# Batch 1 of a retention-and-mixer kernel: all token blocks mixed by token and turned by DMA, its last chunk closer, and one chunk's loads later in SyncE's queue

## The chip, the cores and the metric

The kernel runs on one core of a Trainium2 chip. The metric is the device time of one execution in microseconds. Every time below is of one core; the TensorE clock granted in the profiled execution was 1.000 of full speed.

## What is computed

Two stages in a row. The first is a recurrent attention over 4 batches, 8 heads, 768 tokens and 64 channels a head: a state of 64 x 64 per head decays by gamma at each token. The second mixes the tokens through a rank of 32 and then applies a two-layer MLP (512 to 2048 to 512) to every token.

```python
def _attn_ref(q, k, v):
    gamma = 1.0 - 2.0 ** (-5.0 - np.arange(H))
    for t in range(S):
        state = gamma[None, :, None, None] * state + np.einsum('bhd,bhe->bhde', k[:, :, t], v[:, :, t])
        y[:, :, t] = scale * np.einsum('bhd,bhde->bhe', q[:, :, t], state)

def _moe_ref(x, U, V, w_ch1, w_ch2):
    xt = x.transpose(0, 2, 1)
    h = xt @ U @ V
    u = x + h.transpose(0, 2, 1)
    ch = np.maximum(u @ w_ch1, 0.0) @ w_ch2
    return u + ch
```

x is the attention's output with the heads side by side (768 tokens x 512), the inputs q, k, v are float32, and so is the output.

## The kernel before

**Tiles and stages.** The 768 tokens of a batch are six chunks (or token blocks) of 128. The attention of a chunk takes the decay into q and k (GpSimd: kd at L250, qd at L255), turns both (qkT, channels on partitions), forms the scores of the chunk (ret_S: 8 matmuls, then two masks a on VectorE, L440), adds the product with the state of the chunks before (ret_O, with x cast on ScalarE, L459), and carries the state on (L478, VectorE). Batches 0 and 1 turn q and k on TensorE (ret_T, L418), batches 2 and 3 by DMA transposes (ret_T_dma, L281, two to a chunk, on SyncE's queue).

**The mixer.** mix_P forms P = U^T x (six matmuls). u = x + V^T P exists in two forms. By token (mix_n): one matmul of 512 columns on TensorE, an add of x on VectorE into the float32 tile res (L530), a cast to bf16 on ScalarE (L532), and one DMA transpose of 128 x 512 into the tile uT on SyncE's queue (L534). By channel (mix_u): three turns of x and one matmul of P and V (384 columns) accumulate one channel block of uT for three token blocks in PSUM, and one eviction writes it; then the residual u is formed again at the end of MLP2 (in mlp2 one more matmul of Vb and P_sb of 512 columns, and x added). by_token(b, j) says which form token block j of batch b takes: in the kernel before, batch 0 none, batch 1 blocks 3 to 5, batches 2 and 3 all.

**The MLP.** MLP1 makes 32 pieces of gT (16 row blocks m times 2 halves of 384 tokens, four matmuls of 384 columns each, 0.65 us). For b > 0 the list of slots starts with eight pieces of the first half of tokens and then eight of the second. mlp1_two runs two pieces together, channel blocks 0 and 1 of both first, then 2 and 3. MLP2 makes, for each of six token blocks j, 16 matmuls of 512 columns in eight slots of two; the last adds the residual on VectorE (L575) and stores 128 x 512 from SyncE (L578).

**What sets the order.** Every engine runs its own instructions strictly in the order of the program. The loop over b at the end of the program builds the main list: MLP1(b), 32 slots, then MLP2(b), 48 slots; n1 is the first slot of MLP2. Into it go, at slots given by hand, the attention of batch b + 1 (at: the turns, S_at: the scores, O_at: the outputs) and its mixer (mix_at: mix_P two slots later, then mix_n and mix_u). For batch 1 these slots lie in MLP2 of batch 0, for batches 2 and 3 in MLP1 and the first part of MLP2 of the batch before. Which of ScalarE and VectorE evicts a piece is chosen while the program is built, by an estimate of their loads (Balance.pick).

**SyncE's queue** holds, in program order, the loads of k, q and v (load_one, L135, 256 KB each), the stores and all DMA transposes; an instruction that waits holds up all behind it. Loads of batch b + 1 are issued at the places of ret_in (batch 1's chunks named in EARLY load one chunk of batch 2 each) and at slots 0, 7 and 15 of MLP1.

Of the kernel before, what the change touches and what calls it, by code (L numbers as in the profile page):

```python
# [47 lines left out]
def kernel(  # L48
# [14 lines left out]
    NCK = S // P  # L63
# [4 lines left out]
    NCB = DM // P  # L68
# [37 lines left out]
    def mm_bank(who="main"):  # L106
        if use[who] is None:
            who = "main"
        b = use[who][n_use[who] % len(use[who])]
        n_use[who] += 1  # L110
        taken[b] = n_bank[0]
        return bank(b)

    def matmul(o, l, r, cols, **kw):
        nc.tensor.matmul(o, l, r, **kw)  # L115
        bal.mm(cols)

    def evict(o, i, cols, relu=False, dve_rate=1.0):
        if bal.pick(cols, dve_rate) == "A":
            nc.scalar.activation(o, i, AF.Relu if relu else AF.Copy)  # L120
        elif relu:
            nc.vector.tensor_relu(o, i)
        else:
            nc.vector.tensor_copy(out=o, in_=i)  # L124
# [13 lines left out]
    def load_chunk(b, c, kinds="kqv"):  # L138
        t = staged.setdefault((b, c), {})
        for nm in kinds:  # L140
            load_one(t, b, c, {"k": k, "q": q, "v": v}[nm], nm + "_n")
# [26 lines left out]
    for what in ("q0", "kA", "q1", "k2", "k3", "vA", "q2", "k4", "v2", "k5", "v3", "v4", "v5"):  # L168
        src, i = {"q": q, "k": k, "v": v}[what[0]], what[1]
# [83 lines left out]
    def ret_q(b, c, eng):  # L253
        qd = rmid.tile([P, H, D], bf16, tag="qd", name=f"qd_{b}_{c}", bufs=4)
        eng.tensor_tensor(qd, rc[b, c]["q_n"], Gq[:, c].unsqueeze(2).to_broadcast([P, H, D]),  # L255
                          op=ALU.mult)
        rc[b, c]["qd"] = qd
# [5 lines left out]
        rc[b, c]["vb"] = vb  # L263


    EARLY = (2, 3, 4)

    def ret_in(b, c):
        ret_k(b, c, nc.gpsimd)
        ret_q(b, c, nc.gpsimd)  # L270
        if b == 1 and c in EARLY:
            load_chunk(b + 1, c - EARLY[0])

# [223 lines left out]
    def mix_x(b, hf, c, bk=None):  # L497
        pieces[b, hf, c] = piece = (mm_bank("mix") if bk is None else bank(bk))[:, :HS]
        for jj in range(HS // P):
            j = hf * (HS // P) + jj  # L500
            matmul(piece[:, ts(jj, P)], xs[b][:, j, ts(c, P)], ident, P, start=(jj == 0),
                   stop=False, skip_group_check=True)

    def mix_h(b, hf, c):
        piece = pieces.pop((b, hf, c))
        matmul(piece, Ps[b][:, ts(c, P)], Vb[:, ts(hf, HS)], HS, start=False, stop=True,
               skip_group_check=True)
        evict(uTs[b][:, c, ts(hf, HS)], piece, HS)

    def mix_u(b, hf, c):  # L510
        mix_x(b, hf, c)
        mix_h(b, hf, c)
# [3 lines left out]
    res = {}  # L516

    def by_token(b, j):
        return b >= 2 or (b == 1 and j >= NCK // 2)

    def res_of(b):
        if b not in res:
            res[b] = resp.tile([P, NCK, DM], fp32, tag="res", name=f"res_{b}")
        return res[b]

    def mix_n(b, j):
        h = mm_bank("mix")
        matmul(h, Vb[:, ts(j, P)], Ps[b], DM, start=True, stop=True)
        u = res_of(b)[:, j]
        nc.vector.tensor_tensor(u, h, xs[b][:, j], op=ALU.add)  # L530
        bal.book("V", 0.69)
        nc.scalar.activation(xs[b][:, j], u, AF.Copy)  # L532
        bal.book("A", 0.63)
        nc.sync.dma_start_transpose(out=uTs[b][:, :, ts(j, P)], in_=xs[b][:, j])  # L534
# [11 lines left out]
    def mlp1_two(b, ms, hf):  # L546
        if b not in gTs:
            gTs[b] = gtp.tile([P, NM, S], bf16, tag="gT", name=f"gT_{b}")
        g = [mm_bank()[:, :HS] for _ in ms]
        for cs in ((0, 1), (2, 3)):  # L550
            for m, o in zip(ms, g):
                for c in cs:
                    matmul(o, w1b[:, c, ts(m, P)], uTs[b][:, c, ts(hf, HS)], HS, start=(c == 0),
                           stop=(c == NCB - 1))
        for m, o in zip(ms, g):
            evict(gTs[b][:, m, ts(hf, HS)], o, HS, relu=True)
# [43 lines left out]
    def put(side, i, f):  # L600
        side.setdefault(int(i), []).append(f)
# [17 lines left out]
    def mix_side(b, i, side):  # L619
        put(side, i + 2, lambda: mix_P(b))  # L620
        js = [j for j in range(NCK) if by_token(b, j)]
        for n, j in enumerate(js):
            put(side, i + 5 + n, lambda j=j: mix_n(b, j))
        if b == 1:
            for c in range(NCB):
                put(side, i + 5 + len(js) + c, lambda c=c: mix_u(b, 0, c))
        return side


# [55 lines left out]
    for b in range(B):  # L685
        nxt = b + 1 < B
        slots = mlp1_slots(b)
        n1 = len(slots)
        side = {}
        set_banks([0, 1, 2, SA, SB, OB])  # L690
        if b == 0:
            taken.update({i: n for n, i in enumerate((1, 2, 0, OB, SA, SB, TP))})
            set_banks([1, 2, 0, OB, SA, SB, TP])
            slots[:4] = [lambda: mlp1_two(0, (0, 1), 0), lambda: None,
                         lambda: mlp1_two(0, (0, 1), 1), lambda: None]
            for i, s in ((1, 2), (2, 3)):
                put(side, i, lambda s=s: load_w1(512 * s, 512))
            for s in range(4):
                put(side, 4 + s, lambda s=s: load_w2(s))
            for c, nm in ((0, "kq"), (1, "kq"), (2, "kq"), (0, "v"), (3, "kq"), (1, "v"), (4, "kq"),  # L700
                          (2, "v"), (3, "v"), (5, "kq"), (4, "v"), (5, "v")):
                put(side, 14, lambda c=c, nm=nm: load_chunk(1, c, nm))
            at, lead, mix_at = [n1 + 7 + 5 * c for c in range(NCK)], 4, n1 + 38
            S_at = {(0, 1): n1 + 14, (2, 3): n1 + 24, (4,): n1 + 30, (5,): n1 + 35}
            O_at = [n1 + i for i in (19, 22, 29, 32, 35, 38)]
        if b:

            slots = slots[:16:2] + slots[1:16:2] + slots[16:]
        if b == 1:
            slots[:2] = [lambda: mlp1_two(1, (0, 1), 0), lambda: None]  # L710
        if b and nxt:
            set_banks([0, 1, 2])
            at, lead, mix_at = [10 + 4 * c for c in range(NCK)], 5, n1 + 25
            S_at = {(0, 1): 27, (2, 3): 37, (4, 5): 47}
            O_at = [32, 35, 43, 46, 53, 56]
        if nxt:
            ret_side(b + 1, at, lead, S_at, O_at, side)
            put(side, n1, lambda: set_banks([0, 1], [2]))
            put(side, mix_at, lambda: use.update(mix=[2, SA, SB, OB]))
            mix_side(b + 1, mix_at, side)  # L720
        if b in (1, 2):
            for c, i in ((3, 0), (4, 7), (5, 15)):
                put(side, i, lambda c=c: load_chunk(b + 1, c))
        weave(slots + mlp2_slots(b), side)

# [29 lines left out]
```

## Time and profile before

| | |
|---|---|
| median of 3 runs | 226.94 us (226.93 to 226.95) |
| the profiled execution's own time | 226.93 us |
| its span, first to last instruction | 225.2 us |
| VectorE, ScalarE, GpSimd busy | 38%, 50%, 26% of the span |
| DMA moved | 34.85 MB, 155 GB/s over the span |
| DMA transposes | 15 into uT, 24 into qkT |

How to read the rows that follow: a row of the timeline gives the start in us from the span's first instruction, how long it lasts, the engine (PE is TensorE, PEld its weight load, DVE VectorE, ACT ScalarE, POOL GpSimd, SPq the issue of a DMA by SyncE), the source line, the operation, what is written and read, how many were merged (x), and in brackets the idle time before with what ended it. A matmul's time runs from its issue to its modelled end, and the next one starts before that end, so the distance of starts is what a matmul costs. An SPq row is the time that SyncE is held by the issue, not the transfer; the transfer's end is given by the time "to landing". DMA share is the mean busy share of the core's 16 DMA engines, where overlapping packets can make more than 1.

### The profile page before, as it was taken

What the parts mean: (1) busy time and instruction counts of PE and PEld (TensorE: products, weight loads), DVE (VectorE), ACT (ScalarE), POOL (GpSimd) and SP (SyncE); (2) the same over time, 40 slices, a digit from 0 to 9 for tenths busy, and PEclk for the clock granted to TensorE, in tenths of its full rate; (3) what the DMA queues carried; (4) which work ended last, traced back from release to release, by engine and by line L of the source; (5) the groups of instructions that cost most, each with busy time, mean ns of one, the idle gap of its engine ahead of it and who ended that gap; (6) DMA issues with size and microseconds to landing.
All of it is one profiled execution on the core that took longest, in us unless ns stands there. A gap on an engine that the chain in (4) does not pass through costs nothing.

```text
span 225.2 us, 4288 instructions
## 1 busy us (share of the span) xinstructions
PE 219.7 (98%) x1735; PEld 124.7 (55%) x1735; DVE 85.4 (38%) x163; ACT 112.0 (50%) x220; POOL 58.9 (26%) x66
## 2 busy tenths in 40 slices
PE   7998999999999999999999999999999999999994
PEld 2466655655656466556554456565554455654454
DVE  8597630003777450034673610045674410001221
ACT  3377657751355277767133547776323467760000
POOL 6756920046643431431035103330000000000000
PEclk9999999999999999999999999999999999999999
DMA  6998999999899999989499669995311580001212
GB/s 172 243 265 181 162 189 199 198 223 226 186 232 219 234 232 206 201 168 127 101 210 243 196 134 231 174 187 97 93 49 57 131 143 0 0 3 47 88 52 95
DMA packets 100772, 34.85 MB, mean 155 GB/s; under 512 B 87152, under 2 KB 97808, under 8 KB 100752
## 3 DMA queue, kind: packets, MB, share of 16 engines
q1 hardware_dynamic: 94640, 30.29, 66.0%
q0 software_dynamic: 6112, 4.29, 13.0%
q8 instruction: 13, 0.21, 0.4%
q14 instruction: 7, 0.06, 0.1%
HBM read 27.46 MB, written 6.29 MB: 150 GB/s over the span
## 4 chain that ended last, share of the span: by engine, by line
PE 90%; DMA 3%; POOL 2%; DVE 1%; ACT 1%; SPq 0%; issue 0%; ACTq 0%
PE bk L115 88%; DMA in<-in_q_dram 3%; POOL qd L304 1%; PE bk L418 1%; ACT st L292 1%; PE bk L311 1%; DVE a L345 1%; SPq L165 0%; POOL kd L299 0%; DVE kT L294 0%; PE bk L323 0%; DVE vb L294 0%; DVE res L575 0%; ACTq L292 0%
## 5 line engine op out<-in xcount | busy, mean ns | idle before, releaser
L115 PE MATMUL bk<-w2b,gT 128*128 128x512 bf16 (+2 forms) x416 | 92.0, 363 | 0.0
L115 PE MATMUL bk<-uT,w1b 128*128 128x384 bf16 x512 | 84.3, 326 | 0.0
L120 ACT ACTIVATE gT<-bk 128x384 bf16<-128x384 f32 x123 | 60.4, 491 | 31.8 <-PE bk L115 31.8
L115 PEld LDWEIGHTS <-w1b 128*128 128x128 bf16 x512 | 49.9, 98 | 33.3 <-issue 0.2
L115 PEld LDWEIGHTS <-gT 128*128 128x128 bf16 x416 | 37.9, 98 | 37.8 <-issue 0.8
L250 POOL TENSOR_TENSOR kd<-k_n,Gk 128x512 bf16<-128x512 f32 x18 | 18.8, 1042 | 77.8 <-DMA k_n<-in_k_dram 58.7
L440 DVE TENSOR_TENSOR a<-bk,mask 128x512 bf16<-128x512 f32 x36 | 22.4, 683 | 36.0 <-PE bk L115 35.8
L575 DVE TENSOR_TENSOR res<-bk,res 128x512 f32<-128x512 f32 (+2 forms) x17 | 10.6, 626 | 44.6 <-PE bk L115 44.6
L459 ACT ACTIVATE x<-bk 128x512 bf16<-128x512 f32 x18 | 10.7, 595 | 23.3 <-PE bk L115 23.3
L255 POOL TENSOR_TENSOR qd<-q_n,Gq 128x512 bf16<-128x512 f32 x18 | 18.8, 1042 | 6.8 <-DMA qkT<-qd 3.4
L478 DVE TENSOR_TENSOR state<-bk,bmask 128x512 bf16<-128x512 f32 x15 | 10.4, 691 | 10.7 <-PE bk L115 10.7
L261 ACT ACTIVATE vb<-v_n 128x512 bf16<-128x512 f32 x18 | 10.8, 622 | 5.8 <-DMA v_n<-in_v_dram 5.8
L530 DVE TENSOR_TENSOR res<-bk,x 128x512 f32<-128x512 f32 x15 | 9.7, 685 | 8.4 <-PE bk L115 8.4
L532 ACT ACTIVATE x<-res 128x512 bf16<-128x512 f32 x15 | 9.3, 630 | 7.1 <-DVE res L530 6.9
L115 PEld LDWEIGHTS <-qkT 64*128 64x128 bf16 (+1 forms) x204 | 8.4, 95 | 7.1 <-issue 3.2
L115 PE MATMUL bk<-idle 128*128 128x512 bf16 x29 | 10.3, 499 | 1.2 <-DVE idle L179 1.2
L124 DVE COPY qkT<-bk 128x1024 bf16<-128x1024 bf16 x3 | 2.1, 691 | 23.9 <-PE bk L418 23.9
L115 PE MATMUL bk<-vb,a 128*128 128x64 bf16 (+1 forms) x208 | 10.1, 193 | 0.0
L115 PE MATMUL bk<-P_sb,Vb 128*128 128x512 bf16 x24 | 9.1, 380 | 0.0
L115 PEld LDWEIGHTS <-a 128*128 128x128 bf16 (+1 forms) x208 | 8.5, 97 | 0.7
L115 PE MATMUL bk<-vb,kd 128*128 128x128 bf16 (+1 forms) x88 | 8.2, 219 | 0.2 <-DVE vb L294 0.2
L345 DVE TENSOR_TENSOR a<-bk,mask 128x512 bf16<-128x512 f32 x12 | 7.7, 684 | 1.4 <-PE bk L115 1.4
(85 smaller groups left out, 132.0 us busy)
## 6 DMA issues: line engine op xcount, KB each, us to landing
out_dram<-res SPq DMA_DIRECT2D x23, 256.0 KB, 2.4
k_n<-in_k_dram SPq DMA_DIRECT2D x22, 256.0 KB, 5.0
v_n<-in_v_dram SPq DMA_DIRECT2D x22, 256.0 KB, 5.0
q_n<-in_q_dram SPq DMA_DIRECT2D x18, 256.0 KB, 5.1
w2b<-in_moe_w_ch_dram POOLq DMA_DIRECT2D x4, 512.0 KB, 15.0
in<-in_q_dram SPq DMA_DIRECT2D x3, 512.0 KB, 6.3
w1b<-in_moe_w_ch_dram POOLq DMA_DIRECT2D x4, 256.0 KB, 6.0
w1b<-in_moe_w_ch_dram POOLq DMA_DIRECT2D x2, 512.0 KB, 9.2
```

The lines of the kernel that those rows point to most:

```text
L115: nc.tensor.matmul(o, l, r, **kw)
L120: nc.scalar.activation(o, i, AF.Relu if relu else AF.Copy)
L250: eng.tensor_tensor(kd, k_n, Gk[:, c].unsqueeze(2).to_broadcast([P, H, D]), op=ALU.mult)
L255: eng.tensor_tensor(qd, rc[b, c]["q_n"], Gq[:, c].unsqueeze(2).to_broadcast([P, H, D]), op=ALU.mult)
L261: nc.scalar.activation(vb, rc[b, c]["v_n"], AF.Copy)
L345: nc.vector.tensor_tensor(r0["a", c][:, e], r0["s", c][e].rearrange("p (n t) -> p n t", n=NP), mask0[:, c].unsqueeze(1).to_broadcast([P, N ...
L440: nc.vector.tensor_tensor(r["a"][:, e], r["s"][e].rearrange("p (n t) -> p n t", n=NP), mask4, op=ALU.mult)
L459: nc.scalar.activation(xs[b][:, c], o, AF.Copy)
L478: nc.vector.tensor_tensor(sb, ps.rearrange("p (n t) -> p n t", n=NP), bmask4, op=ALU.mult)
L530: nc.vector.tensor_tensor(u, h, xs[b][:, j], op=ALU.add)
L532: nc.scalar.activation(xs[b][:, j], u, AF.Copy)
L575: nc.vector.tensor_tensor(o, chp.pop((b, j)), o if by_token(b, j) else xs[b][:, j, ds(lo, w)], op=ALU.add)
```

## The change

Four things change. (1) by_token takes all six blocks of batch 1: blocks 0 to 2 go through mix_n as 3 to 5 did, the four mix_u of batch 1 are gone, and MLP2 of batch 1 adds the finished u instead of forming it again with a matmul for blocks 0 to 2. The two paired MLP1 pieces at the start of MLP1 of batch 1 are single ones again. (2) The last chunk of batch 1 comes earlier: turn at slot n1 + 31 (32 before), scores and the output of chunk 4 at n1 + 34 (35), the output of chunk 5 at n1 + 36 (38). (3) mix_at goes from n1 + 38 to n1 + 36 and the first mix_n follows four slots behind instead of five. (4) The loads of chunk 2 of batch 2 leave the place of batch 1's chunk 4 and go to slot 0 of MLP1 of batch 1, chunk 3's from slot 0 to slot 2.

```diff
-    EARLY = (2, 3, 4)
+    EARLY = (2, 3)
...
     def by_token(b, j):
-        return b >= 2 or (b == 1 and j >= NCK // 2)
+        return b >= 1
...
         for n, j in enumerate(js):
-            put(side, i + 5 + n, lambda j=j: mix_n(b, j))
-        if b == 1:
-            for c in range(NCB):
-                put(side, i + 5 + len(js) + c, lambda c=c: mix_u(b, 0, c))
+            put(side, i + (4 if b == 1 else 5) + n, lambda j=j: mix_n(b, j))
...
-            at, lead, mix_at = [n1 + 7 + 5 * c for c in range(NCK)], 4, n1 + 38
-            S_at = {(0, 1): n1 + 14, (2, 3): n1 + 24, (4,): n1 + 30, (5,): n1 + 35}
-            O_at = [n1 + i for i in (19, 22, 29, 32, 35, 38)]
+            at, lead, mix_at = [n1 + i for i in (7, 12, 17, 22, 27, 31)], 4, n1 + 36
+            S_at = {(0, 1): n1 + 14, (2, 3): n1 + 24, (4,): n1 + 30, (5,): n1 + 34}
+            O_at = [n1 + i for i in (19, 22, 29, 32, 34, 36)]
...
-        if b == 1:
-            slots[:2] = [lambda: mlp1_two(1, (0, 1), 0), lambda: None]
...
-            for c, i in ((3, 0), (4, 7), (5, 15)):
+            for c, i in ((2, 0), (3, 2), (4, 7), (5, 15)) if b == 1 else ((3, 0), (4, 7), (5, 15)):
                 put(side, i, lambda c=c: load_chunk(b + 1, c))
```

SyncE's queue at the end of MLP2 of batch 0, before. res_901 is batch 0's output, x_1008 and uT_1288 are batch 1's, k_n_2 to v_n_4 are chunks 2 to 4 of batch 2:

```order
L135 DMA k_n_2_1069<-in_k_dram 128x8x64
L135 DMA q_n_2_1071<-in_q_dram 128x8x64
L135 DMA v_n_2_1073<-in_v_dram 128x8x64
L578 DMA out_dram<-res_901 128x512 x3
L534 DMA_TRANSPOSE uT_1288<-x_1008 128x4x128 x3
L578 DMA out_dram<-res_901 128x512
L135 DMA k_n_3_1349<-in_k_dram 128x8x64
L135 DMA q_n_3_1351<-in_q_dram 128x8x64
L135 DMA v_n_3_1353<-in_v_dram 128x8x64
L135 DMA k_n_4_1402<-in_k_dram 128x8x64
L135 DMA q_n_4_1404<-in_q_dram 128x8x64
L135 DMA v_n_4_1406<-in_v_dram 128x8x64
```

The same place in the changed kernel (res_901 is still batch 0's output, uT_1276 batch 1's):

```order
L578 DMA out_dram<-res_901 128x512 x3
L534 DMA_TRANSPOSE uT_1276<-x_1008 128x4x128 x6
L578 DMA out_dram<-res_901 128x512
L135 DMA k_n_2_1334<-in_k_dram 128x8x64
L135 DMA q_n_2_1336<-in_q_dram 128x8x64
L135 DMA v_n_2_1338<-in_v_dram 128x8x64
L135 DMA k_n_3_1353<-in_k_dram 128x8x64
L135 DMA q_n_3_1355<-in_q_dram 128x8x64
L135 DMA v_n_3_1357<-in_v_dram 128x8x64
L135 DMA k_n_4_1393<-in_k_dram 128x8x64
L135 DMA q_n_4_1395<-in_q_dram 128x8x64
L135 DMA v_n_4_1397<-in_v_dram 128x8x64
```

Three transposes more stand between the stores, and the three loads of chunk 2 moved from ahead of the stores to behind the transposes; in both kernels the four transposes of q and k of batch 2's chunks 0 and 1 follow, then chunk 5's loads and the transposes of chunks 2 to 5.

VectorE at the same place, before (state_4 is the last state of batch 1, res_1299 its u by token):

```order
L478 TENSOR_TENSOR state_4_1251<-bk_95_1018,bmask 128x512
L575 TENSOR_TENSOR res_901<-bk_109_1210,x_391 128x512
L530 TENSOR_TENSOR res_1299<-bk_116_1297,x_1008 128x512
L530 TENSOR_TENSOR res_1299<-bk_117_1305,x_1008 128x512
L530 TENSOR_TENSOR res_1299<-bk_118_1312,x_1008 128x512
L575 TENSOR_TENSOR res_901<-bk_115_1289,x_391 128x512
L124 CAST uT_1288<-bk_122_1343 128x384
```

and in the changed kernel (res_1285 is batch 1's u by token):

```order
L478 TENSOR_TENSOR state_4_1243<-bk_95_1018,bmask 128x512
L575 TENSOR_TENSOR res_901<-bk_109_1204,x_391 128x512
L530 TENSOR_TENSOR res_1285<-bk_115_1283,x_1008 128x512
L530 TENSOR_TENSOR res_1285<-bk_117_1293,x_1008 128x512
L530 TENSOR_TENSOR res_1285<-bk_118_1300,x_1008 128x512
L530 TENSOR_TENSOR res_1285<-bk_119_1307,x_1008 128x512
L530 TENSOR_TENSOR res_1285<-bk_120_1314,x_1008 128x512
L530 TENSOR_TENSOR res_1285<-bk_121_1321,x_1008 128x512
L575 TENSOR_TENSOR res_901<-bk_116_1289,x_391 128x512
```

The adds are six instead of three, the cast of a mix_u piece is gone, and the residual of batch 0's token block 4 (bk_109) stands directly ahead of the first add in both. On TensorE the first mix_n stood after block 4 and six matmuls of block 5 of MLP2; now it stands right behind block 4's last matmul. From there to the first matmul of MLP1 of batch 1 TensorE has 23 matmuls of 512 columns (six mix_n, one Vb with P_sb, sixteen of w2b).

## The prediction

> **What bounds the kernel now.** I read the page first, then the chain of waits, then the timeline from 70 to 115 us, where every moved instruction lies.
>
> ```profile
> span 225.2 us, 4288 instructions
> PE 219.7 (98%) x1735; PEld 124.7 (55%) x1735; DVE 85.4 (38%) x163; ACT 112.0 (50%) x220; POOL 58.9 (26%) x66
> ```
>
> The columns are busy us, share of the span and instructions. TensorE (PE) leaves only 5.5 us of the span. The chain of waits in order of time (start, us, what) ends so:
>
> ```profile
> 69.41 152.68 PE bk L115 x1114
> 222.09 0.02 issue
> 222.11 0.29 DVE res L575
> ```
>
> From 69 us on the chain is TensorE alone: 1114 matmuls and no wait. So a matmul that is dropped is time gained, and a wait put between two matmuls is time lost, unless a later wait swallows it. All times below are times of this profiled execution. Its own time is 226.93 us (span 225.2 and 1.73 around it), 0.01 under the median of 226.94, so differences carry over as they are.
>
> **What TensorE saves.** The timeline where MLP2 of batch 0 hands over to MLP1 of batch 1 (start us, busy us, engine, line):
>
> ```profile
> 75.33 0.61 PE L115 MATMUL bk<-x,Ub 128*32 128x512 bf16 x6
> 75.87 0.39 PE L115 MATMUL bk<-P_sb,Vb 128*128 128x512 bf16 x1
> 77.39 0.38 PE L115 MATMUL bk<-P_sb,Vb 128*128 128x512 bf16 x1
> 77.81 2.06 DVE L530 TENSOR_TENSOR res<-bk,x 128x512 f32<-128x512 f32 x3 [1.61 <-PE bk L115]
> 78.54 1.99 ACT L532 ACTIVATE x<-res 128x512 bf16<-128x512 f32 x3 [1.93 <-DVE res L530]
> 79.59 4.66 SPq L534 DMA_TRANSPOSE uT<-x  x3
> 79.67 0.59 PE L115 MATMUL bk<-w2b,gT 128*128 128x512 bf16 x2
> 80.43 0.59 PE L115 MATMUL bk<-w2b,gT 128*128 128x512 bf16 x2
> 81.52 8.78 PE L115 MATMUL bk<-uT,w1b 128*128 128x384 bf16 x53
> ```
>
> From 75.87 to 77.39 stand seven matmuls of 512 columns: 0.217 us each. From 79.67 to 80.43 stand two of these and one mix_u (three turns and one matmul of 384 columns): 0.76 - 0.43 = 0.33 us. Four mix_u go: **-1.33 us**. The three new mix_n cost 0.217 each here, and three matmuls Vb, P_sb of the same size go from MLP2 of batch 1: nil in the sum, but 0.65 is paid before MLP1 and returned after it. The four evictions that go, and the three adds (0.69) and casts (0.66) that come, run on VectorE and ScalarE, 38% and 50% busy: nothing by themselves.
>
> **The last chunk drawn together.** In the timeline:
>
> ```profile
> 71.53 0.40 PE L115 MATMUL bk<-qkT 64*128 64x128 bf16 x8
> 72.56 1.46 PE L115 MATMUL bk<-w2b,gT 128*128 128x512 bf16 x6
> 73.17 0.68 DVE L478 TENSOR_TENSOR state<-bk,bmask 128x512 bf16<-128x512 f32 x1
> 73.91 0.40 PE L115 MATMUL bk<-state,qkT 128*128 128x128 bf16 x4
> ```
>
> From the scores of chunk 5 (71.53) to its output (73.91) VectorE needs 2.38 us for two masks and the state. The six matmuls between end at 73.86, so TensorE waits 0.05 today. The change leaves four there: it comes 0.43 earlier to the same state and waits, **+0.43 us**. The end of mix_P, with all of token block 4 of MLP2 done, goes from 75.87 to 76.30, where mix_n of block 0 now stands.
>
> **MLP1 of batch 1 now waits.** Before, its first half of tokens (columns 0 to 383 of uT) came from mix_u; now it needs the transposes of blocks 0, 1 and 2. VectorE must first finish the residual of block 4, whose last matmul starts at 76.08; a matmul's result is taken 0.42 later (77.39 to 77.81), so 76.50 to 77.19. Then the add of block 0 to 77.88, the cast to 78.55 (78.54 stands 0.73 behind 77.81, and lasts 0.63), the transpose from **78.6**. The adds follow at 0.69, faster than the transposes:
>
> ```profile
> 123.97 2.50 SPq L534 DMA_TRANSPOSE uT<-x  x2
> 127.20 5.77 SPq L534 DMA_TRANSPOSE uT<-x  x4
> DMA to landing us min/median/max: 2.4/2.5/5.1
> ```
>
> These are batch 2's six (issue times on SyncE) and, from the view of tile uT, the time from issue to landing of all fifteen. The third is issued 2.55 after the first, 81.15, and lands 2.5 later: **83.65**. TensorE gets there at 76.30 + 23 x 0.217 = 81.28 and waits 2.4 us. MLP1 starts at 83.7 against 81.52, **+2.2**. Bounds: landing by 2.4 gives +2.1, by 5.1 (under load, as batch 1's own three did) +4.8. The second half of the tokens is needed 32 matmuls of 0.166 (8.78 / 53) later, at 89.0; the sixth transpose, issued near 85.5, lands at 88.0 to 90.6: hidden, or 1.7 more, which the next wait takes up.
>
> A rule speaks on this price. The Trainium skill, in DMA: Bandwidth & Descriptors (Latency and other measured facts), gives a DMA transpose 261 GB/s; by it one of 128x512 bf16, 131 kB, would take 0.50 us, an estimate. The row above has 1.25 us, and the sum uses the row.
>
> **SyncE's queue is late for batch 2.** The transposes of q and k of batch 2 stand behind all this. Timeline, SyncE and TensorE:
>
> ```profile
> 84.36 0.52 SPq L578 DMA_DIRECT2D out_dram<-res  x1
> 85.41 0.39 SPq L135 DMA_DIRECT2D k_n<-in_k_dram  x1
> 87.43 1.02 SPq L135 DMA_DIRECT2D k_n<-in_k_dram  x1
> 91.00 1.78 SPq L281 DMA_TRANSPOSE qkT<-qd  x1
> 95.44 1.26 SPq L281 DMA_TRANSPOSE qkT<-kd  x1
> 99.17 0.62 PE L115 MATMUL bk<-qkT 64*128 64x128 bf16 x16
> 103.44 0.38 PE L115 MATMUL bk<-P_sb,Vb 128*128 128x512 bf16 x1
> 103.79 1.27 SPq L281 DMA_TRANSPOSE qkT<-kd  x1
> 106.59 0.62 PE L115 MATMUL bk<-qkT 64*128 64x128 bf16 x16
> 109.04 1.27 SPq L281 DMA_TRANSPOSE qkT<-kd  x1
> 113.14 0.62 PE L115 MATMUL bk<-qkT 64*128 64x128 bf16 x16
> ```
>
> The three PE rows of qkT are the scores of batch 2's chunks (0,1), (2,3), (4,5); the last transposes for them are issued at 95.44, 103.79 and 109.04 and land 2.5 later, at 97.94, 106.29 and 111.54. The slack today is 1.2, **0.3** and 1.6 us. And the queue does not idle: of SyncE's waits from 91 to 100 us there is one,
>
> ```profile
> SPq L281 <- POOL qd L255: 0.3, 1, 0.3
> ```
>
> so what is put ahead delays all that follows. In the new order: six transposes from 78.6, 2.50 + 5.77 + 0.05, to 86.9; the store, 0.57 (84.36 to the end of its issue) to 1.05 (to the next row, 85.41), I take 0.8, to 87.7; nine loads, the first three at 2.02 (85.41 to 87.43), the next six at 3.57 each three (87.43 to 91.00), 9.16 in all, to **96.9**. That is 5.9 later than 91.00, and TensorE is only 2.2 later. Landing for chunks (0,1): 96.9 + 4.44 + 2.5 = 103.8, TensorE there at 101.4: waits 2.4. For (2,3): 96.9 + 12.79 + 2.5 = 112.2; TensorE at 106.59 + 2.2 + 2.4 - 0.22 (the matmul of 103.44 gone) = 111.0: waits 1.2. For (4,5): 117.4 against 118.5: none. Chunk 2's loads stood ahead of the three stores before; behind them they cost 2 to 3.6 us of a full queue. GpSimd's products of chunk 2 wait for them:
>
> ```profile
> k_n<-in_k_dram SPq DMA_DIRECT2D x22, 256.0 KB, 5.0
> ```
>
> 5.0 us from issue, so near 93, and their transposes stand in the queue behind those of chunks 0 and 1 and three more loads, after 102: covered.
>
> **The sum.** The scores of (2,3) start at 112.2 instead of 106.59, +5.6; two more dropped matmuls return 0.43. **+5.1 us, 232.0 us.** The same by parts: -1.33 + 0.43 + 2.4 + 2.4 + 1.2 = +5.1 (the state's wait, MLP1's, and those of the scores (0,1) and (2,3)). The queue decides it, so an error in MLP1's wait is taken up by the next. Bounds of the queue: all nine loads at the pace of the first three (0.67 each) end 3.1 earlier and the store 0.2, +1.8; six transposes at the 1.55 of batch 1's three (4.66 / 3), nine loads at 1.19 and the store at 1.05 give +7.9.
>
> **Rivals.**
>
> A, the queue recovers: batch 2's transposes arrive in time, and only MLP1's wait stands. Time +2.2 - 0.65 = +1.55, 228.5. It decides if the nine loads need 5.5 us or less (0.6 each). For it: less is in flight at 87 us than before. Against it: the second three took 3.57 with the same start, and the DMA engines are full there (share above 1, last columns: TensorE clock, DMA share, GB/s):
>
> ```profile
> 86.00:90.00 4.00, 4.00 (x27) 2.38 (x26) 0.00 (x0) 3.05 (x7) 0.99 (x1) 1.00 1.03 203
> 90.00:94.00 4.00, 4.00 (x26) 2.42 (x25) 0.00 (x0) 2.96 (x7) 2.14 (x3) 1.00 1.35 217
> ```
>
> B, not slower: the issue time of a transpose is only back-pressure, and with chunk 2's loads out of the way it issues as a store does, 0.5 us (0.52 at 84.36). Then the third lands at 78.6 + 1.0 + 2.4 = 82.0, TensorE waits 0.7, the queue reaches q at 91.4 and no score waits: -1.33 + 0.43 + 0.7 = -0.2, 226.7; with a landing 0.5 sooner, 226.2. Below 0.45 apart it turns the sign. Against it: batch 2's took 1.25 each (2.50 for two). The 261 GB/s of the Trainium skill's DMA: Bandwidth & Descriptors would be this rival's pace.
>
> C, TensorE cools: after waits of 2.4 us it restarts slow. At the start of the program it does run slow:
>
> ```profile
> 1.19 6.94 PE L115 MATMUL bk<-idle 128*128 128x512 bf16 x18 [1.19 <-DVE idle L179]
> ```
>
> 0.39 us a matmul against 0.217. If some 3.4 us (half of that stretch) run at half rate behind a wait, it costs 1.7; behind MLP1's wait the next wait hides it, behind the scores' it does not: 233.7. Against it: such waits are short, and no row of before has one. The Trainium skill, in TensorE: Matmul & The Clock Gate (Part 1: The HAM clock gate), asks for an idle window of about 3.4 us before the clock halves, which would leave the sum.
>
> That the change does not do what it says is excluded by the order of the instructions.
>
> **How the numbers follow.** Forecast (both kinds of wait) 0.73, its own range 230 to 233.3; A 0.11; B 0.09, half of it faster; C 0.07. This kernel's measurements tell 0.2%, 0.45 us, from no change. Range 228.4 to 233.6: it reaches down to A, and leaves out B and what lies beyond C at the top. Faster 0.06, within 0.2% 0.04, slower 0.90.
>
> **What would show it.** Right: TensorE idle 2 to 3 us ahead of MLP1 of batch 1, released by the DMA of uT; the first qkT transpose of batch 2 near 97; idle ahead of the scores of (0,1) and (2,3), released by qkT. Wrong: transposes at 0.5 us, the nine loads under 6 us, or MLP1 of batch 1 starting before 82.

## The result, and the profile after

| | before | after |
|---|---|---|
| median | 226.94 us | 233.42 us |
| all runs | 226.93 to 226.95 | 233.02, 233.28, 233.55, 233.62 |
| mean granted TensorE clock | 1.0 (profiled; 0.998 to 1.0 in its runs beside the experiments) | 1.0, 1.0, 0.993, 0.992 |

The ratio of after to before is 1.0283, with a 95% interval of 1.0268 to 1.0298: the change costs 6.5 us. The profiled execution of after is the one of 233.02 us, at full clock.

The page of after, busy us and share of the span:

```profile
span 231.2 us, 4251 instructions
PE 217.0 (94%) x1700; PEld 123.3 (53%) x1719; DVE 87.0 (38%) x165; ACT 112.6 (49%) x220; POOL 59.1 (26%) x66
```

TensorE does 2.7 us less work (217.0 for 219.7; some of that may be records that are missing) in a span 6.0 longer. What it waits for from 60 us on, where the kernel before has no row at all (us in total, times, longest):

```profile
PE bk L115 <- DMA qkT<-kd: 3.9, 4, 1.5
PE bk L115 <- DMA uT<-x: 2.4, 1, 2.4
PE bk L115 <- DVE state L478: 0.3, 1, 0.3
PE bk L115 <- issue: 0.3, 2, 0.2
```

The first three rows are waits of the kind predicted: the transposes of q and k, those of u, and the state. The two of 0.16 us under "issue" stand where one of twelve matmuls is missing from the trace. The timeline of TensorE has them one by one (in brackets the idle time before, and what ended it):

```profile
73.54 0.40 PE L115 MATMUL bk<-state,qkT 128*128 128x128 bf16 x4 [0.33 <-DVE state L478]
83.92 17.71 PE L115 MATMUL bk<-uT,w1b 128*128 128x384 bf16 x108 [2.40 <-DMA uT<-x]
102.20 0.40 PE L115 MATMUL bk<-qkT 64*128 64x128 bf16 x8 [0.58 <-DMA qkT<-kd]
104.14 0.40 PE L115 MATMUL bk<-qkT 64*128 64x128 bf16 x8 [1.54 <-DMA qkT<-kd]
111.13 0.40 PE L115 MATMUL bk<-qkT 64*128 64x128 bf16 x8
112.71 0.40 PE L115 MATMUL bk<-qkT 64*128 64x128 bf16 x8 [1.19 <-DMA qkT<-kd]
118.82 0.62 PE L115 MATMUL bk<-qkT 64*128 64x128 bf16 x16
162.58 0.40 PE L115 MATMUL bk<-qkT 64*128 64x128 bf16 x8 [0.62 <-DMA qkT<-kd]
```

And SyncE's queue, whose rows answer them:

```profile
78.63 8.55 SPq L534 DMA_TRANSPOSE uT<-x  x6
87.29 0.52 SPq L578 DMA_DIRECT2D out_dram<-res  x1
88.32 0.39 SPq L135 DMA_DIRECT2D k_n<-in_k_dram  x1
97.23 1.73 SPq L281 DMA_TRANSPOSE qkT<-qd  x1
101.62 1.26 SPq L281 DMA_TRANSPOSE qkT<-kd  x1
110.16 1.28 SPq L281 DMA_TRANSPOSE qkT<-kd  x1
140.29 2.49 SPq L135 DMA_DIRECT2D v_n<-in_v_dram  x1
158.69 2.44 SPq L281 DMA_TRANSPOSE qkT<-kd  x1
```

The six transposes of u take 8.55 us of issuing, the nine loads 88.32 to 97.23, and the first q transpose of batch 2 stands at 97.23 where it was at 91.00. A wait costs more than its bracket. From 111.13 to 112.71 are 1.58 us; eight score matmuls without a wait take 0.22 (16 of them end 0.62 after their start, 8 of them 0.40); 1.36 are lost, and the bracket says 1.19. The idle time counts from the modelled end of the matmul before, which the next one would have overlapped by 0.16 to 0.17. Five waits of 0.33, 2.40, 0.58, 1.54 and 1.19, each with 0.16, are 6.84; less the 1.33 of the four mix_u that is 5.5 us, and MLP1 of batch 2 starts 5.47 later:

```profile
131.24 11.05 PE L115 MATMUL bk<-uT,w1b 128*128 128x384 bf16 x67
```

before, and after:

```profile
136.71 5.53 PE L115 MATMUL bk<-uT,w1b 128*128 128x384 bf16 x33
```

The wait of 0.62 in batch 3's scores (2,3) adds 0.78; the end of the kernel gives 0.26 back. Together 6.0, the difference of the spans. The other three runs lie 0.3 to 0.6 us above the profiled one. The two highest have a lower clock; the third, 233.28, is at 1.0.

### The profile page after: what moved, and what is told of

Read it like the earlier page. It is cut to its first block, busy times and chain, and to the rows that moved or that the text cites. A ratio compares the mean times of both kernels' runs of the same rounds, so it can differ in the third digit from the quotient of the medians.

```text
span 231.2 us, 4251 instructions
## 1 busy us (share of the span) xinstructions
PE 217.0 (94%) x1700; PEld 123.3 (53%) x1719; DVE 87.0 (38%) x165; ACT 112.6 (49%) x220; POOL 59.1 (26%) x66
## 4 chain that ended last, share of the span: by engine, by line
PE 62%; SPq 15%; DMA 12%; ACT 3%; DVE 3%; issue 2%; POOL 1%; POOLq 0%; DVEq 0%
PE bk L115 61%; DMA k_n<-in_k_dram 7%; SPq L281 6%; SPq L135 4%; DMA qkT<-kd 3%; ACT x L532 2%; SPq L165 2%; SPq L534 2%; DMA q_n<-in_q_dram 2%; PE bk L418 1%; DVE res L530 1%; DMA uT<-x 1%; SPq L578 1%; DVE res L575 1%; DVE state L478 1%
## 5 line engine op out<-in xcount | busy, mean ns | idle before, releaser
L115 PE MATMUL bk<-w2b,gT 128*128 128x512 bf16 (+2 forms) x398 | 90.1, 362 | 1.3 <-issue 0.5
L440 DVE TENSOR_TENSOR a<-bk,mask 128x512 bf16<-128x512 f32 x36 | 22.6, 684 | 40.6 <-PE bk L115 40.4
L575 DVE TENSOR_TENSOR res<-bk,res 128x512 f32<-128x512 f32 (+2 forms) x20 | 12.7, 636 | 45.8 <-PE bk L115 45.8
L532 ACT ACTIVATE x<-res 128x512 bf16<-128x512 f32 x18 | 11.1, 630 | 6.5 <-DVE res L530 6.3
L530 DVE TENSOR_TENSOR res<-bk,x 128x512 f32<-128x512 f32 x18 | 11.5, 685 | 6.3 <-PE bk L115 3.1
L124 DVE COPY qkT<-bk 128x1024 bf16<-128x1024 bf16 x4 | 2.8, 689 | 23.9 <-PE bk L418 23.9
L115 PE MATMUL bk<-idle 128*128 128x512 bf16 x28 | 9.0, 457 | 1.2 <-DVE idle L179 1.2
L115 PE MATMUL bk<-qkT 64*128 64x128 bf16 x144 | 6.3, 218 | 3.9 <-DMA qkT<-kd 3.9
```

Of the source, the lines that this page charges most:

```text
L440: nc.vector.tensor_tensor(r["a"][:, e], r["s"][e].rearrange("p (n t) -> p n t", n=NP), mask4, op=ALU.mult)
L575: nc.vector.tensor_tensor(o, chp.pop((b, j)), o if by_token(b, j) else xs[b][:, j, ds(lo, w)], op=ALU.add)
```

## The experiments

The theory that went into them, Q: the time is TensorE's waits, set by two chains, the one through the first half of u (mix, add, cast, three transposes, landing), the other through SyncE's queue, in which what is put ahead delays q and k of batch 2. The rivals: the waits are only where the loss shows, and an edit alone would show it elsewhere; and TensorE's clock takes a part.

**The parts of the change alone.** Four kernels: the change without its part 4; the kernel before with part 4 alone; with part 1 alone; with part 2 alone. Part 3 (mix_P and the first mix_n earlier) was not run by itself.

```diff
after, part 4 undone:
-    EARLY = (2, 3)
+    EARLY = (2, 3, 4)
-            for c, i in ((2, 0), (3, 2), (4, 7), (5, 15)) if b == 1 else ((3, 0), (4, 7), (5, 15)):
+            for c, i in ((3, 0), (4, 7), (5, 15)):
before, part 4 alone: these two the other way round
before, part 1 alone:
-        return b >= 2 or (b == 1 and j >= NCK // 2)
+        return b >= 1
-        if b == 1:
-            for c in range(NCB):
-                put(side, i + 5 + len(js) + c, lambda c=c: mix_u(b, 0, c))
-            slots[:2] = [lambda: mlp1_two(1, (0, 1), 0), lambda: None]
before, the last chunk alone (at, S_at, O_at as in the change, mix_at left at n1 + 38)
```

> The changed kernel with part 4 undone (chunk 2's loads ahead of the stores again). Theory Q (SyncE's queue sets when batch 2's scores can start, MLP1's wait is set by the third transpose of u): the six transposes start later and land under load, as batch 1's three did before (3.2 to 5.1 us), so MLP1 of batch 1 starts near 86.5 and waits about 5 us instead of 2.4; q's first transpose comes at 94 to 95 instead of 97.2 and the scores of batch 2 wait little or not. Sum 231 to 232.5 us, below the changed kernel's 233.4. Rival M (only MLP1's wait counts, it stays 2.4 us): the scores' waits go and nothing comes in their place, 229 to 229.5. Rival L (the loads' place does not matter): 233.4.

> The kernel before with part 4 alone. Theory Q: no wait at MLP1 of batch 1; q's first transpose of batch 2 at about 93 instead of 91.0, the scores of (0,1) wait about 0.7 and those of (2,3) about 1 us: 228.5 to 229. Rival M: no wait ahead of the scores, 226.9 to 227.1. Rival L: 226.94.

> The kernel before with part 1 alone (all blocks of batch 1 by token, the paired pieces of MLP1 single), mix_n still five slots behind mix_P and the last chunk where it was. Theory Q: the first transpose starts at 79.6 under chunk 2's loads, MLP1 of batch 1 starts at 85.5 to 87 and waits 4.5 to 6 us; the queue behind has six transposes but not the loads, and the scores of batch 2 wait little or not: 230.2 to 232. Rival M: wait of 3.5 us at most, 229.3. Rival B of the prediction (a transpose issues in 0.5 us): 227 to 228.

> The kernel before with part 2 alone (last chunk of batch 1 drawn together, mix_P where it was). All theories: TensorE waits 0.3 to 0.45 us for the last state and nothing else moves: 227.25 to 227.4. If the earlier P is worth something by itself: 226.9 or below.

| kernel | median, us | runs (mean clock) | ratio to before, 95% |
|---|---|---|---|
| change without part 4 | 231.88 | 230.12 (1.0), 230.89 (0.993), 232.87 (0.984), 232.95 (0.984) | 1.0196 [1.0138, 1.0253] |
| part 4 alone | 230.32 | 229.65 (0.998), 230.27 (0.998), 230.38 (1.0), 230.48 (0.991) | 1.0146 [1.013, 1.0162] |
| part 1 alone | 231.47 | 230.67 (1.0), 231.36 (0.992), 231.58 (0.993), 232.76 (0.984) | 1.0208 [1.0172, 1.0243] |
| last chunk alone | 227.36 | 227.29 to 227.5 (0.999 to 1.0) | 1.0018 [1.0009, 1.0028] |

The last chunk alone costs 0.4 us and its profile has the state's wait of 0.33 (with 0.16, 0.49). In the medians, which hold losses by the clock too, parts 1 and 4 each cost 3 to 5 us alone, 8 with the last chunk's, and 6.5 together. That fits a score that waits for the queue and so does not wait once more for what came late before it.

Of Q's four forecasts only the last chunk's came out whole. Part 4 alone missed its time (228.5 to 229 said, 230.32 measured). Part 1 alone has its time in the range, but its wait at MLP1 is 3.69 us where 4.5 to 6 were said, and three of its four runs lost some clock. The change without part 4 has its time in the range by luck: MLP1 waits 3.55 us and not about 5, and a slower TensorE makes up the difference. The timeline of that kernel, and TensorE's clock by stretches (us, busy us, granted clock, DMA share, GB/s):

```profile
84.94 20.57 PE L115 MATMUL bk<-uT,w1b 128*128 128x384 bf16 x108 [3.55 <-DMA uT<-x]
105.44 0.62 PE L115 MATMUL bk<-qkT 64*128 64x128 bf16 x16
```

```profile
84.00:86.00 2.00, 1.06 (x4) 0.50 0.48 95
86.00:88.00 2.00, 2.00 (x8) 0.50 0.67 73
90.00:92.00 2.00, 2.00 (x11) 0.80 0.96 231
```

The 108 matmuls take 20.57 us where after has 17.71: 2.86 more, at half the clock from 84 to some way past 90. The scores then need not wait for the queue, since TensorE comes late itself. Part 4 alone shows the same behind a wait of only 1.76 us:

```profile
101.24 0.40 PE L115 MATMUL bk<-qkT 64*128 64x128 bf16 x8 [1.76 <-DMA qkT<-kd]
101.57 5.10 PE L115 MATMUL bk<-uT,w1b 128*128 128x384 bf16 x20
```

```profile
102.00:104.00 2.00, 2.00 (x7) 0.50 1.30 263
104.00:106.00 2.00, 2.00 (x10) 0.73 1.55 148
```

But part 1 alone waits longest of the four, 3.69 us, and in its profiled execution nothing follows:

```profile
84.74 5.36 PE L115 MATMUL bk<-uT,w1b 128*128 128x384 bf16 x32 [3.69 <-DMA uT<-x]
```

(32 matmuls at 0.163 and the end of the last, 5.36: full speed.) So the clock came in as a second cause, one that strikes in some executions. Theory H: a wait of some 2 us can bring the clock down to half for a while afterwards.

**TensorE kept busy through the waits.** Matmuls on data that nothing reads, put into the places of waiting. They add work and shorten no wait, so that only the clock can gain as long as nothing else moves.

```diff
change without part 4:
+        if b == 1:
+            put(side, 0, lambda: run_idle(16, ST))
part 4 alone:
+        if b == 1:
+            put(side, 27, lambda: run_idle(8, ST))
the change itself:
+        if b == 1:
+            put(side, 0, lambda: run_idle(11, ST))
+            put(side, 27, lambda: run_idle(8, ST))
+            put(side, 37, lambda: run_idle(5, SA))
```

> The change without its part 4 (chunk 4's heads made early again, chunk 2 loaded early), and 16 matmuls of 512 columns on data that nothing reads, put ahead of the first MLP1 matmul of batch 1; they add work and leave the waits as they are. In the run without them this matmul waited 3.55 us for the transposed u, MLP1 then took 20.57 us where it takes 17.71 undisturbed, with a granted clock of 0.50 for some 6 us, and the runs lay between 230.1 and 233.0. Theory (an idle TensorE is granted half its clock for some us afterwards): with TensorE kept busy through the wait no such stretch follows, every run has a clock of 1.0 at this place and the time is 230.1 to 230.5, spread below 0.5. Rival (the clock drops for another reason, with load alone or by chance): MLP1 is as slow in some runs as before, the runs keep a spread of 1 to 3 us, and the time is 231 to 233. Second rival (the matmuls outlast the wait or delay the u): MLP1 starts later than 85, 231 with little spread.

> The kernel before with part 4 alone (chunk 2 of batch 2 loaded in MLP1), and 8 matmuls of 512 columns on data that nothing reads ahead of the scores of batch 2's chunks 0 and 1, which waited 1.76 us there; the following 5.10 us of MLP1 took 3.42 undisturbed, at a granted clock of 0.50. Clock theory: with TensorE busy through that wait the clock stays at 1.0, and the time is 230.3 - 1.7 = 228.4 to 228.9 in every run. Rival (the clock falls with the load of the other engines or by chance, not from the idle time): 230.0 to 230.5 as without them.

> The change as it is, with matmuls of 512 columns on data that nothing reads put into its three places of waiting: 11 ahead of the first MLP1 matmul of batch 1, 8 and 5 ahead of the scores of batch 2's chunks 0, 1 and 2, 3. Clock theory: the runs of the change that lay above its profiled one (233.3 to 233.6 at 0.992 and 0.993, against 233.02 at 1.0) did so through the clock alone, and here all lie between 232.4 and 233.1 at a clock of 1.0. Rival (the spread has another cause): 233.0 to 233.7 as before. If the matmuls outlast the waits: up to 0.5 more in all runs.

| kernel | without, us | with, us | ratio to before, with |
|---|---|---|---|
| change without part 4 | 231.88 (230.12 to 232.95) | 230.28 (229.85 to 230.40) | 1.0139 [1.012, 1.0159] |
| part 4 alone | 230.32 (229.65 to 230.48) | 230.02 (229.62 to 230.11) | 1.0135 [1.0118, 1.0152] |
| the change | 233.42 (233.02 to 233.62) | 232.74 (232.59 to 233.51) | 1.0261 [1.0243, 1.0279] |

The first is what H said. MLP1 starts at 85.29, even later than the 84.94 without, and is 1.6 us faster in the median; every run has a clock of 1.0, and the one run without them that kept its clock took 230.12:

```profile
81.37 3.62 PE L115 MATMUL bk<-idle 128*128 128x512 bf16 x16
85.29 17.71 PE L115 MATMUL bk<-uT,w1b 128*128 128x384 bf16 x108 [0.31 <-DMA uT<-x]
```

The second missed: 0.3 us gained, where about 1.7 were expected; the time is the one that the rival named. The clock held, against the rival: its 20 matmuls are back at 3.42 us. But the next scores now wait for the queue:

```profile
99.23 1.67 PE L115 MATMUL bk<-idle 128*128 128x512 bf16 x7
101.39 3.42 PE L115 MATMUL bk<-uT,w1b 128*128 128x384 bf16 x20
109.50 0.40 PE L115 MATMUL bk<-qkT 64*128 64x128 bf16 x8 [0.84 <-DMA qkT<-kd]
```

With the half clock TensorE came 1.7 us later to these scores and had no wait. A lower clock ahead of a wait is partly hidden by it, and the price of part 4 alone was underrated for this second wait (0.84 and 0.16), not for the clock. Besides, the 1.7 us were taken off a median that hardly held them: three of the four runs without the idle matmuls had a clock of 0.998 to 1.0 already (229.65 to 230.38).

The third gains 0.7 in the median and has three runs of four under 232.9, but its fourth is 233.51 at a clock of 1.0, so not all of the change's spread is the clock. The gain of its profiled run (232.62 at 0.998, against 233.02 at 1.0) is not the clock's either:

```profile
137.07 17.73 PE L115 MATMUL bk<-uT,w1b 128*128 128x384 bf16 x108
186.15 20.96 PE L115 MATMUL bk<-uT,w1b 128*128 128x384 bf16 x128
```

MLP1 of batch 2 starts 0.36 later than in the change (136.71) and MLP1 of batch 3 0.42 earlier (186.57 there), because batch 3's scores do not wait in this execution.

Between them these three kernels and the next one with such matmuls have 16 runs, none with a mean clock under 0.998. The eight kernels with waits of over 1.5 us and nothing to fill them (the change among them) have 32 runs, 17 of them at 0.984 to 0.993. The kernel before is at 0.998 to 1.0 in every run; one of its runs beside the kernel with two queues took 228.81 us at 1.0, for a cause that is not known.

**The order of SyncE's queue.** The change with the loads of chunks 3 to 5 later, so that q and k of chunks 0 and 1 go first; and the same with 11 idle matmuls ahead of MLP1.

```diff
-            for c, i in ((2, 0), (3, 2), (4, 7), (5, 15)) if b == 1 else ((3, 0), (4, 7), (5, 15)):
+            for c, i in ((2, 0), (3, 15), (4, 19), (5, 23)) if b == 1 else ((3, 0), (4, 7), (5, 15)):
```

> The change with the loads of batch 2's chunks 3, 4 and 5 put later in MLP1 of batch 1 (at the 15th, 19th and 23rd slot in place of the 2nd, 7th and 15th), so that in SyncE's queue the q and k transposes of chunks 0 and 1 stand ahead of the loads of chunks 3 and 4. Theory of the prediction (queue order makes the scores of batch 2 late): the first q transpose issues near 90.5 in place of 97.2, scores (0,1) and (2,3) wait 0 to 0.4 in place of 0.58 + 1.54 and 1.19, MLP1's wait of 2.4 stays, and the time is 233.4 - 3.3 to - 4.5 = 228.7 to 230.2. Rival (the loads only push the delay on): the k transposes of chunks 2 to 5 or the v of chunks 3 to 5 are late instead, new waits of 1 to 3 us at scores (4,5) or the outputs of batch 2, 231 to 233. If the place of the loads is not the cause at all: 233.4.

> The kernel with the later loads and 11 matmuls of 512 columns on data that nothing reads ahead of the first MLP1 matmul of batch 1, which waits 2.4 us there. They do not shorten the wait. Clock theory: any run of the kernel with the later loads that lies above its fastest does so by a lower granted clock after this wait; here all lie together at its fastest, 228.7 to 229.3. Rival (the waits alone make the time): the same time as without them, with the same spread, or up to 0.5 more where they outlast the wait.

| kernel | median, us | runs (mean clock) | ratio to before, 95% |
|---|---|---|---|
| later loads | 231.11 | 230.99 (0.999), 231.0 (1.0), 231.22 (1.0), 233.90 (0.993) | 1.0211 [1.0145, 1.0277] |
| with idle matmuls | 230.59 | 230.47, 230.47, 230.72, 230.91 (0.999 to 1.0) | 1.0161 [1.0145, 1.0177] |

The profiled run of the first is the one of 233.90. Its waits and queue:

```profile
83.73 17.82 PE L115 MATMUL bk<-uT,w1b 128*128 128x384 bf16 x108 [2.40 <-DMA uT<-x]
110.08 0.40 PE L115 MATMUL bk<-qkT 64*128 64x128 bf16 x8 [1.00 <-DMA qkT<-kd]
118.55 0.40 PE L115 MATMUL bk<-qkT 64*128 64x128 bf16 x8 [1.96 <-DMA qkT<-kd]
118.88 4.45 PE L115 MATMUL bk<-w2b,gT 128*128 128x512 bf16 x12
```

```profile
91.00 1.60 SPq L281 DMA_TRANSPOSE qkT<-qd  x1
104.15 3.35 SPq L281 DMA_TRANSPOSE qkT<-qd  x1
116.02 1.27 SPq L281 DMA_TRANSPOSE qkT<-kd  x1
```

The queue theory holds for the place of the wait: the first q transpose is at 91.00 instead of 97.23 and the scores (0,1), which waited 2.12 us in two pieces, do not wait. The rival holds for the sum: the last k transpose comes at 116.02 instead of 115.41, and the scores (4,5), which did not wait, wait 1.96. So 2.3 us are gained in the median and not 3.3 to 4.5. And this execution lost clock too: 12 matmuls at 118.88 take 4.45 us, where 2.76 is the time of 11 or 12 elsewhere. That is 1.69 of the 2.7 to 2.9 us by which it lies above the other three runs, of which there is no profile. With the idle matmuls at MLP1 the four runs lie within 0.44 us, as the clock theory said, but at 230.59 and not at 228.7 to 229.3, which rested on the forecast that had just failed. The wait at the scores (4,5), 1.89 in the profile of this kernel, stays unfilled; none of its four runs lost the clock there, which four runs cannot exclude for the next.

**A shorter way to u.** VectorE adds straight into the bf16 x of batch 1, so that the cast falls away (the residual of batch 1 is then the bf16 u); mix_P over chunks 0 to 4 runs a slot before that of chunk 5; chunks 4 and 5 are drawn two slots earlier; the end of one output block of batch 0 comes behind the mix. To this kernel then two edits: chunk 2 of batch 2 loaded ahead of the mix again, and the loads of chunks 2 and 4 issued by ScalarE. Both place the remaining loads anew as well: chunks 3 to 5 at slots 0, 15 and 19 in the first, chunks 2 to 5 at 2, 15, 17 and 21 in the second (2 to 5 at 0, 15, 19 and 23 in the kernel that they change).

```diff
earlier u, on top of the later loads:
+        if b == 1:
+            nc.vector.tensor_tensor(xs[b][:, j], h, xs[b][:, j], op=ALU.add)
+            nc.sync.dma_start_transpose(out=uTs[b][:, :, ts(j, P)], in_=xs[b][:, j])
+            return
...
+            put(side, i + 1, lambda: mix_P(b, (0, 1, 2, 3, 4)))
+            put(side, i + 2, lambda: mix_P(b, (5,)))
...
-            at, lead, mix_at = [n1 + i for i in (7, 12, 17, 22, 27, 31)], 4, n1 + 36
+            at, lead, mix_at = [n1 + i for i in (7, 12, 17, 22, 25, 29)], 4, n1 + 34
chunk 2 ahead of the mix:
-    EARLY = (2, 3)
+    EARLY = (2, 3, 4)
two queues:
-        nc.sync.dma_start(
+        (nc.scalar if b == 2 and c in (2, 4) else nc.sync).dma_start(
```

> A try at a version faster than both: the change with the later loads, and the u of batch 1 taken earlier: VectorE adds it straight into the bf16 x, so that no cast stands between it and its transpose (the residual of batch 1 is then the bf16 u); the mixing matmul over chunks 0 to 4 runs one slot ahead of that of chunk 5; the last two chunks' q and k are drawn two slots earlier; and the end of one output block of batch 0 is put off behind the mix. Theory (what is left of the loss is MLP1's wait for the last of the transposes of the first half): the wait shrinks from 2.4 to 0.5 or less, and the time is 226.0 to 227.0, about the kernel before or just under it. Rival (the transposes stand behind each other on SyncE whatever the u does, each 1.4 us): the wait stays above 1.5, 228 to 229.

> The kernel with the earlier u, with chunk 2 of batch 2 loaded ahead of the mix again (its loads fall on SyncE's queue between 71 and 75, ahead of two stores and of the transposes of u), and in MLP1 of batch 1 only the loads of chunks 3, 4 and 5 (at the first, the 15th and the 19th slot). With the loads inside MLP1 the scores (4,5) waited 1.89 us and (2,3) 0.32, with MLP1's own wait 0.47. Theory (SyncE's queue in MLP1 is too long by one chunk's loads, about 2.5 us): both waits go, MLP1 waits 0.5 to 1.3, span 226.0 to 227.2, time 227.8 to 229.0, still not under the kernel before. Rival (the loads ahead of the mix delay the transposes of u by their whole length): MLP1 waits over 2 us, 229.5 to 231.

> The kernel with the earlier u and the later loads, with the loads of batch 2's chunks 2 and 4 issued by ScalarE in place of SyncE, at the 2nd and 17th slot of MLP1 of batch 1 (chunk 3 at the 15th and chunk 5 at the 21st slot stay with SyncE). With all in SyncE's queue its profile had MLP1 wait 0.47, scores (2,3) 0.32, scores (4,5) 1.89 and batch 3's scores (2,3) 0.57, and a time of 230.53 at full clock. Theory (it is SyncE's issuing that is full, about 1.2 us for a transpose and 2.3 for a chunk's three loads, and not the transfers): the waits of (2,3) and (4,5) go to 0 to 0.4, time 228.2 to 229.0. Rival 1 (the DMA engines' own traffic sets when transposes land): these waits stay, 230 to 231. Rival 2 (ScalarE is held up by issuing loads, its ReLU evictions come late): TensorE waits on ScalarE in MLP1, 229 to 232.

| kernel | median, us | runs (mean clock) | ratio to before, 95% |
|---|---|---|---|
| earlier u | 230.91 | 230.53 (0.999), 230.87 (0.999), 230.95 (1.0), 232.23 (0.993) | 1.0192 [1.0154, 1.023] |
| chunk 2 ahead of the mix | 230.26 | 228.93 (0.998), 229.19 (1.0), 231.33 (0.993), 231.65 (0.993) | 1.0145 [1.0088, 1.0202] |
| two queues | 237.19 | 236.32 (0.992) to 237.47 (0.986) | 1.043 [1.0375, 1.0485] |

The earlier u was expected to bring the time to 226.0 to 227.0 and missed by some 4 us. It does what it should to MLP1's wait and no more:

```profile
82.63 17.71 PE L115 MATMUL bk<-uT,w1b 128*128 128x384 bf16 x108 [0.47 <-DMA uT<-x]
108.19 0.40 PE L115 MATMUL bk<-qkT 64*128 64x128 bf16 x8 [0.32 <-DMA qkT<-kd]
116.59 0.40 PE L115 MATMUL bk<-qkT 64*128 64x128 bf16 x8 [1.89 <-DMA qkT<-kd]
```

So the wait for u is a chain that can be shortened; the rival, that it stays above 1.5 us whatever the u does, falls. The transposes' own distance stays a part of the chain: the first is issued at 77.31, 1.32 earlier than in the change, and MLP1 starts 1.29 earlier. (The rest of the shorter wait is TensorE, which reaches MLP1 at 82.16 and not at 81.52.) What is gained at MLP1 comes back at the scores (4,5), whose transposes still stand behind all the loads in SyncE's queue. Putting chunk 2's loads ahead of the mix removes that wait and brings back MLP1's, as the rival had it, because the two stores that follow the loads then end at 79.3 and the transposes start at 79.38 instead of 77.31:

```profile
73.83 0.95 SPq L135 DMA_DIRECT2D k_n<-in_k_dram  x1
77.37 1.91 SPq L590 DMA_DIRECT2D out_dram<-res  x2
79.38 8.37 SPq L536 DMA_TRANSPOSE uT<-x  x6
```

```profile
84.67 19.16 PE L115 MATMUL bk<-uT,w1b 128*128 128x384 bf16 x108 [2.49 <-DMA uT<-x]
```

Its runs lie in two pairs: 229.06 at full clock (the mean of two) and 231.49 with half the clock for a while. Of these 2.4 us the slow MLP1 is 1.45 (19.16 for 17.71). The profiled run, one of the slow pair, also waits 0.78 us in batch 3's scores; whether the fast pair does is not known, as neither of it was profiled. Even at full clock this kernel is 2.1 us over the kernel before. The second queue was worse, in the way of rival 2 but far beyond its 229 to 232, and for a reason that was not foreseen:

```profile
84.19 0.43 ACTq L135 DMA_DIRECT2D k_n<-in_k_dram  x1
89.13 0.38 ACTq L135 DMA_DIRECT2D q_n<-in_q_dram  x1
90.96 0.39 ACTq L135 DMA_DIRECT2D v_n<-in_v_dram  x1
91.39 1.25 ACT L120 ACTIVATE gT<-bk 128x384 bf16<-128x384 f32 x3 [6.78 <-DMA qkT<-qd]
```

The program gives its DMAs eight completion counters in turn, over both queues, and each issue waits for the DMA that had the counter before it. The order of the instructions, with what each waits for:

```
ScalarE
L135 DMA k_n_2_1340<-in_k_dram 128x8x64 [waits DMAHW2_49,Pool_49]
L135 DMA q_n_2_1342<-in_q_dram 128x8x64 [waits DMAHW7_49,Pool_49]
L135 DMA v_n_2_1344<-in_v_dram 128x8x64 [waits DMAHW1_49,DMAHW0_49,Activation_49]
```

Counter 7 was last that of the store at 86.53 and counter 1 that of the first q transpose at 88.06 on SyncE; so q went at 89.13 and v at 90.96, and the ReLUs behind them (the evictions of MLP1's pieces) stood for 6.78 us. TensorE waited 5.90 for one, and its clock was 0.50 from about 89.2 to 96.1. Whether the transposes would have come in time with a free second queue stays open: no run had one.

No version beats the kernel before.

## Why the prediction was right

The direction, the size within 1.5 us and the places of the waits were right: 232.0 was said, with 230 to 233.3 for this case and 228.4 to 233.6 in all; 233.42 was measured, 233.02 in the profiled execution. The whole range held by only 0.2 us, and the one for this case holds the profiled execution but not the median. Step by step:

- **The four mix_u, -1.33.** It agrees with the sum of the waits up to MLP1 of batch 2 (6.84 - 1.33 = 5.5, measured 5.47); it was not measured by itself.
- **The state, +0.43.** 0.33 idle and 0.16 lost overlap, 0.49 in place of the 0.05 of before, so +0.44; alone the edit costs 0.42 us (227.36 to 226.94).
- **MLP1's wait, 2.4 from a chain of add, cast and transposes.** First transpose at 78.63 (78.6 said), wait 2.40, MLP1 at 83.92 (83.7 said). The chain is right: without the cast, two slots earlier, the wait is 0.47.
- **The queue.** Six transposes 8.55 (8.3), the store to the next row 1.03 (0.8), nine loads 8.91 (9.16), the first q transpose at 97.23 (96.9). Waits of (0,1) 2.12 idle (2.4), of (2,3) 1.19 (1.2), of (4,5) none (none). That the queue's order sets them was shown by the later loads; that an error in MLP1's wait is taken up by the next holds in kind: parts 1 and 4 alone cost 8 us in sum with the last chunk's, 6.5 together.
- **The sum, +5.1.** Measured 5.47 at the same point. With the lost overlap the four terms measured 0.49, 2.56, 2.44 and 1.35, which is 0.04 to 0.16 more each, 0.4 in all.
- **What the sum left out.** Batch 3, of which nothing was said: the largest term that the sum put at nothing. Its scores (2,3) wait 0.62, 0.78 with the overlap. Its q transposes start 6.2 later (146.14 for 139.93) where TensorE is 5.5 later; two SyncE rows of 2.49 and 2.44 us (140.29 and 158.69) lie on the way to the last transpose for these scores. Its slack was never worked out, and the profile of before had it: the transpose issued at 152.79 landed 3.2 later, at 156.0, and the second eight score matmuls stood at 156.3. In after it is issued at 158.69 and lands 3.8 later, at 162.5, where TensorE would have come at 161.8.
- **Rival A, the queue recovers (0.11).** Wrong: nine loads took 8.91, not 5.5.
- **Rival B, a transpose issues at 0.5 us (0.09).** Wrong: no transpose in any profile of these kernels took less than 1.19 us to issue, so that the price of 0.50 estimated from the 261 GB/s in the Trainium skill's DMA: Bandwidth & Descriptors (Latency and other measured facts) is not met here.
- **Rival C, TensorE cools after a wait (0.07).** Underrated. Its mechanism exists, with the price that it named: some 3.4 us at half the clock, 1.7 lost. In the change itself it costs little: its two runs at 0.992 and 0.993 lie 0.3 to 0.6 us above the two at 1.0, which fits a loss that a later wait swallows. Filling the waits gains 0.7 of the 6.5 us in the median, and the profiles show that at least part of this is the wait in batch 3 and not the clock. In the change without part 4 it costs 1.6 in the median and 2.8 between its fastest and its slowest run. The step that failed is the argument against it, "such waits are short", and the use of the idle window of about 3.4 us from the Trainium skill's TensorE: Matmul & The Clock Gate (Part 1: The HAM clock gate), by which the sum was to stay: the clock fell after waits of 1.76, 1.96 and 2.49 us, and here the measurement decides against the page. The same section calls the window free-running. This agrees with what the runs show, that the same kernel keeps its clock in one execution and loses it in the next; it does not by itself explain a fall after a wait shorter than the window, and that stays open.

## What to carry to other kernels

Where one engine is busy for 98% of the span, a change that drops work from it must be priced by the chains that feed it: 1.33 us of matmuls were saved here and 6.8 us of waits put in, all but 0.5 of them behind a queue that had a slack of 0.3 us. The order of a full queue did not mend it here: each reordering moved the wait to another reader (from the scores (0,1) to (4,5), then to MLP1). The slack must be worked out for every later reader of the queue, in the next batch too. And where TensorE had to wait 3.5 us, idle matmuls in that place cost little (MLP1 0.35 us later) and saved 1.6 us in the median by keeping the clock; where a later wait followed, they saved 0.3.

## What the runs showed of the hardware that was not expected

In the stretches that were read in windows of 0.4 us (five kernels that lost clock) the granted clock is 1.0 or 0.50, but for the windows at a switch, where a mean over both explains what lies between. The stretches at 0.50 last some 3.4 or some 6.8 us: 4.45 - 2.76 = 1.69 and 5.10 - 3.42 = 1.68 were lost in two of them, half of 3.4; in the change without part 4 it lasts from about 84.0 to 90.8, with two queues from 89.2 to 96.1. They begin not with the wait but 2 to 3.2 us after its start, even when TensorE works again: the scores of part 4 alone wait from 99.48, resume at 101.24, and the clock falls near 101.7. Why the same wait brings it down in one execution and not in another was not found.

A wait's bracket in the timeline is 0.16 us short of what it costs, for matmuls that follow each other closely: the overlap with the matmul before is lost as well.

Single issues on SyncE last two to three times their usual time in some places (3.35 us for a transpose at 104.15 with the later loads, 2.49 for a load at 140.29 in after, against 1.2 and 1.0). Such an issue can open a wait where the slack is below a microsecond, as in batch 3; what causes them was not tried.
